# Merging two matrices of a linear-attention layer: the order and shape of the block products

## The chip, the cores and the metric

The kernel runs on one core of one Trainium2 chip. The metric is device time in microseconds of one execution. A core has five engines that run beside each other, each through its own list of instructions: TensorE (PE in the profile; its weight loads are PEld), VectorE (DVE), ScalarE (ACT), GpSimd (POOL) and SyncE (SP), which here issues DMA transfers.

## What is computed

Four layers follow one another, A, B, A, B, each over a sequence of 2048 tokens with 640 features in 32 heads of 20. A is a linear-attention layer, B a layer with softmax attention inside four segments of 512 tokens and a memory across them. The change lies in layer A, which both times runs the same code:

```python
def _A_ref(x, wqkv, wo):                       # x is layer-normed
    qkv = (x @ wqkv).reshape(B, S, 3, H, Dh).transpose(2, 0, 3, 1, 4)
    q, k, v = qkv[0], qkv[1], qkv[2]
    phi = lambda t: jnp.where(t > 0, t + 1, jnp.exp(t)) + 1e-6
    pq, pk = phi(q), phi(k)
    kv = jnp.einsum("bhsd,bhse->bhde", pk, v)
    z = jnp.einsum("bhsd->bhd", pk)
    num = jnp.einsum("bhqd,bhde->bhqe", pq, kv)
    den = jnp.einsum("bhqd,bhd->bhq", pq, z)[..., None] + 1e-6
    o = num / den
    return o.transpose(0, 2, 1, 3).reshape(B, S, D) @ wo
```

## The kernel before

Rows are tiled to 128 partitions (P), the 640 features to five tiles of 128 (C), the sequence to four segments of 512. A matrix of high accuracy is held as an upper and a lower 16-bit part, and a product of two such matrices is three products (upper by upper, upper by lower, lower by upper). Results of 640 columns are made in two halves of 320 (HN), each in a bank of PSUM; `bank()` hands out eight banks in turn.

Layer A never projects v. `g_first` goes through the segments, makes phi of the keys and queries, and sums G = (phi of the keys, transposed) x, in `memory`, whose ten parts are five tiles by two halves. In the last segment (s = 3) it calls `merge`, which turns G into one matrix `wm` that stands for the v projection, the keys' memory and the output projection together. Its stages are, in the order of TensorE's list:

- two steps of `fill`, a generator that holds the four halves of the last two query projections, `queries(2)` and `queries(3)`. A half is 15 products (`proj_n`, L430), an exponential and a relu on ScalarE (`phi_a`), two instructions of VectorE (L445, L747) and a store to DRAM (L748);
- two parts of `memory`, the sums of the keys (L821) with their reciprocals, and the other eight parts of `memory`. VectorE scales G (L837), ScalarE makes the upper copy (L839) and VectorE the lower one (L840), first for the first half of the columns, then for the second;
- one step of `fill`;
- the five inner blocks. Block t is `wv` (tile t of rows) times the scaled G for the heads that touch the tile: heads LO[t] to HI[t], 7 or 8 heads, 140 or 160 columns (L858). VectorE masks the result to the heads' own blocks (L864), ScalarE makes the upper copy in `kt` (L867), VectorE the lower one (L868). A `kt` tile has 512 columns, the block stands from column 128 on, and GpSimd writes zeros on both sides of it (L848, L849). Behind block 1 stands the fourth step of `fill`;
- a further step of `fill`, which by then has nothing left;
- the five outer blocks. Block u is the inner blocks times `wo`. Heads of 20 features do not end at multiples of 128, so beside its own inner block (L888, 128 columns of `kt` as the stationary operand) block u takes a strip of 32 columns of its neighbours' blocks (L894): blocks 0 and 4 have one neighbour, blocks 1 to 3 have two, whose strips are the output rows 0 to 31 and 96 to 127. Each of the two halves has three products per operand, so a block has 6 wide products and 6 or 12 narrow ones. Then ScalarE and VectorE write the two parts of `wm` (L897, L898).

Behind it stands the next stage: `a_head` and `a_second` scale the queries (L929, L933 to L937), transpose them (`turn`, L348) and multiply by `wm` (L430). `merge` runs once at the end of the opening, near 195 to 236 us, and once in the middle, near 1016 to 1054 us. The tile `xo` is the layer's input, loaded again for the sum; `w_Bv` is a weight of layer B, fetched into a buffer that `w_Aq` held.

The order of TensorE's list is the order of the program. The other engines' lists are put in order by a scheduler when the program is built. In the opening GpSimd's queue issues the stores of the queries (L748), later SP's; the weights are always fetched by GpSimd's queue (L300).

Of the kernel before, what the change touches and what calls it, by code (L numbers as in the profile page):

```python
# [20 lines left out]
S, D, H, DH = 2048, 640, 32, 20  # L21
P = 128
C = D // P
# [5 lines left out]
HN = 320  # L29
# [5 lines left out]
LO = [(P * t) // DH for t in range(C)]  # L35
HI = [(P * t + P - 1) // DH for t in range(C)]
# [108 lines left out]
class Kernel:  # L145
# [656 lines left out]
    def merge(self, L, wv, wo, memory, fill):  # L802


        nc, sb = self.nc, self.sb

        def filled(k):
            for _ in range(k):
                x = next(fill, None)
                if x:  # L810
                    yield x

        yield from filled(2)
        for _ in range(2):
            yield next(memory)
        zb = L["z"]
        rz = self.row("rz")
        for n in range(2):
            c = slice(n * HN, (n + 1) * HN)
            p = self.bank()[:, :HN]  # L820
            nc.tensor.matmul(p, self.mhalf.to_broadcast([P, P]), L["z"][:, c], start=True, stop=True)  # L821
            nc.vector.tensor_scalar(zb[:, c], p, -2.0, S * 1e-6, op0=OP.mult, op1=OP.add)
            nc.vector.reciprocal(rz[:, c], zb[:, c])
            nc.vector.tensor_scalar(rz[:, c], rz[:, c], self.k_inv, G_ONE, op0=OP.mult, op1=OP.mult)
            yield 4 * HN * COL
        gs, eps = [], sb.tile([P, C], F32, tag="rca", name="eps", bufs=3)
        for n in range(2):
            for _ in range(C - 2 if n == 0 else C):
                yield next(memory)
            t = self.x_t()  # L830
            gs.append(t)
            for c in range(C):
                e = sb.tile([P, SEG], F32, tag="pq", name="ge", bufs=PQ)[:, :HN]
                if n == 0:
                    nc.vector.tensor_scalar(eps[:, c:c + 1], L["G"][c][:, HN:HN + 1], self.k_scl, 1e-6,
                                            op0=OP.mult, op1=OP.mult)
                nc.vector.scalar_tensor_tensor(e, L["G"][c][:, n * (HN + 1):n * (HN + 1) + HN], eps[:, c:c + 1],  # L837
                                               rz[:, n * HN:(n + 1) * HN], op0=OP.add, op1=OP.mult)
                nc.scalar.activation(t[:, c, 0, :HN], e, AF.Copy)  # L839
                L["parted"] = nc.vector.tensor_tensor(t[:, c, 1, :HN], e, t[:, c, 0, :HN], op=OP.subtract)  # L840
        L["zb"] = zb
        L["pre"] = [self.p_load(L, 0, i) for i in range(3)]
        for _ in memory:
            pass
        yield from filled(1)
        kt = [sb.tile([P, 2, SEG], F16, tag="row", name="kt", bufs=ROWS) for _ in range(C)]
        for t, k2 in enumerate(kt):
            nc.gpsimd.memset(k2[:, :, 64:P], 0.0)  # L848
            nc.gpsimd.memset(k2[:, :, P + (HI[t] + 1 - LO[t]) * DH:320], 0.0)  # L849
        for t, k2 in enumerate(kt):  # L850
            p = self.bank()
            lo, hi = LO[t] * DH, (HI[t] + 1) * DH
            first = True
            for n in range(2):
                a, b = max(lo, n * HN), min(hi, (n + 1) * HN)
                for c in range(C if a < b else 0):
                    for k, m in ((0, 0), (0, 1), (1, 0)):
                        nc.tensor.matmul(p[:, a - lo:b - lo], wv[:, c, k, t * P:(t + 1) * P],  # L858
                                         gs[n][:, c, m, a - n * HN:b - n * HN],
                                         start=first, stop=c == C - 1 and k == 1, skip_group_check=True)  # L860
                        first = False
            e = sb.tile([P, 512], F32, tag="er", name="ke", bufs=3)[:, :hi - lo]
            h = "p (h e) -> p h e"
            nc.vector.scalar_tensor_tensor(e.rearrange(h, e=DH), p[:, :hi - lo].rearrange(h, e=DH), V_SHIFT / G_ONE,  # L864
                                           self.blk[:, OFF[t]:OFF[t] + WID[t]].rearrange(h, e=E1)[:, :, :DH],
                                           op0=OP.mult, op1=OP.mult)
            nc.scalar.activation(k2[:, 0, P:P + hi - lo], e, AF.Copy)  # L867
            L["split"] = nc.vector.tensor_tensor(k2[:, 1, P:P + hi - lo], e, k2[:, 0, P:P + hi - lo], op=OP.subtract)  # L868
            yield 15 * (hi - lo) * COL
            if t == 1:  # L870
                yield from filled(1)
        L["kt"] = True
        for v in L["v"]:
            self.ones_column(v)
        wm = sb.tile([P, C, 2, D], F16, tag="wo", name="wm", bufs=2)
        yield from filled(1)
        halves = [slice(n * HN, (n + 1) * HN) for n in range(2)]
        for u in range(C):
            edges = []
            if u > 0 and (HI[u - 1] + 1) * DH > u * P:  # L880
                edges.append((u - 1, slice(0, 32), 32))
            if u < C - 1 and LO[u + 1] * DH < (u + 1) * P:
                edges.append((u + 1, slice(96, 128), 32))
            ps = [self.bank()[:, :HN] for _ in halves]
            for p, c in zip(ps, halves):
                for k, m in ((0, 0), (0, 1), (1, 0)):
                    a = P + u * P - LO[u] * DH
                    nc.tensor.matmul(p, kt[u][:, k, a:a + P], wo[:, u, m, c], start=k == m, stop=k == 1 and not edges,  # L888
                                     skip_group_check=True)
            for p, c in zip(ps, halves):  # L890
                for k, m in ((0, 0), (0, 1), (1, 0)):
                    for t, r, w in edges:
                        a = P + u * P + r.start - LO[t] * DH
                        nc.tensor.matmul(p[r], kt[t][:, k, a:a + w], wo[:, t, m, c], start=False, stop=k == 1,  # L894
                                         skip_group_check=True)
            for p, c in zip(ps, halves):
                nc.scalar.activation(wm[:, u, 0, c], p, AF.Copy, scale=W_SHIFT)  # L897
                nc.vector.scalar_tensor_tensor(wm[:, u, 1, c], p, W_SHIFT, wm[:, u, 0, c],  # L898
                                               op0=OP.mult, op1=OP.subtract)
                yield 6 * HN * COL  # L900
        L["wm"] = wm
        yield from filled(8)
# [640 lines left out]
```

## Time and profile before

| | us |
|---|---|
| median of 3 runs | 1653.96 |
| lowest and highest of them | 1652.17 and 1654.64 |
| the profiled execution | 1653.39 |
| its span, first to last instruction | 1651.40 |
| TensorE busy | 1613.4 |
| VectorE busy | 1239.5 |

The profile is of one execution. Its span is shorter than its time, because the time has some 2 us around the first and the last instruction. The chain of waits is followed back from the last instruction: at each step to what released it, or to the instruction before it on its engine. Each of its pieces is given with its start, the time that it holds of the chain, and its line.

### The profile page before, as it was taken

To read this page: it belongs to the slowest core of one execution; us is meant where nothing else is said; L and a number is where in the kernel's file an instruction comes from. 1 tells how busy PE (TensorE), PEld (TensorE's weight loads), DVE (VectorE), ACT (ScalarE), POOL (GpSimd) and SP (SyncE) were. 2 spreads that over 40 slices of the span, in tenths; PEclk is the share of its full clock that TensorE was granted. 3 is DMA by queue.
4 is the path that set the end of the run, shared out by engine and by line. 5 is a ranking of instruction groups with operands and counts; after the bars stand their busy time and mean duration, and the time that the engine had idled before them with its cause. 6 is when DMAs were issued, how large, how long until landed. Compare 5 with 4: busy or idle time off the path is not lost.

```text
span 1651.4 us, 37827 instructions
## 1 busy us (share of the span) xinstructions
PE 1613.4 (98%) x13772; PEld 1016.8 (62%) x13772; DVE 1239.5 (75%) x4007; ACT 1015.1 (61%) x1955; POOL 493.0 (30%) x1023
## 2 busy tenths in 40 slices
PE   9999999999999999999999999999999999999998
PEld 6777776654665575556567777756546646645555
DVE  8777794788887797768764556838888878878772
ACT  6877743367667656667666544433775675666773
POOL 3421132023223423433341301210232342332552
PEclk9999999999999999999999999999999999999999
DMA  6444743423322432352211303623232232323422
GB/s 225 160 140 161 275 174 100 134 73 111 96 70 81 142 99 95 108 190 69 66 46 52 102 33 128 214 90 120 77 111 91 100 114 93 109 88 112 147 95 97
DMA packets 110346, 189.32 MB, mean 115 GB/s; under 512 B 14160, under 2 KB 69840, under 8 KB 107728
## 3 DMA queue, kind: packets, MB, share of 16 engines
q1 hardware_dynamic: 97536, 141.02, 26.5%
q0 software_dynamic: 3264, 24.91, 4.1%
q10 hardware_dynamic: 9360, 20.98, 3.3%
q8 instruction: 109, 1.79, 0.5%
q14 instruction: 77, 0.63, 0.1%
HBM read 109.32 MB, written 77.00 MB: 113 GB/s over the span
## 4 chain that ended last, share of the span: by engine, by line
PE 83%; DVE 6%; ACT 5%; DMA 2%; issue 2%; POOL 1%; SPq 0%; ACTq 0%; DVEq 0%; POOLq 0%
PE ps L430 35%; PE ps L416 13%; PE ps L1269 8%; PE ps L757 7%; PE ps L1242 4%; PE ps L348 4%; PE ps L1201 3%; ACT pe L1246 3%; PE ps L472 2%; DVE ps L1207 1%; PE ps L1282 1%; PE ps L1046 1%; PE ps L1056 1%; PE ps L894 1%; DVE oT L353 1%
## 5 line engine op out<-in xcount | busy, mean ns | idle before, releaser
L1207 DVE CUSTOM_DVE_ANT_0 ps<-ps,maskw 128x512 f32<-128x512 f32 (+3 forms) x1024 | 472.3, 520 | 47.3 <-PE ps L1201 43.8
L1246 ACT ACTIVATE pe<-ps,lsc 128x512 f32<-128x512 f32 x640 | 391.9, 695 | 86.1 <-PE ps L1242 68.6
L1253 POOL TENSOR_SCALAR_AFFINE_SELECT pe<-pe 128x256 f32<-128x256 f32 (+1 forms) x640 | 238.3, 380 | 371.7 <-ACT pe L1246 368.8
L430 PEld LDWEIGHTS <-xT 128*128 128x128 f16 x2760 | 267.9, 98 | 104.1 <-issue 5.6
L430 PEld LDWEIGHTS <-oT 128*128 128x128 f16 x1920 | 186.4, 98 | 80.7 <-issue 6.3
L1269 PE MATMUL ps<-pe,v 128*32 128x512 f32 (+3 forms) x2048 | 156.7, 436 | 7.4 <-DVE nat L1017 3.5
L1207 DVE DVE_READ_ACCUMULATOR2_ANT mg<- 128x1 f32 x1024 | 144.6, 141 | 0.0
L430 PE MATMUL ps<-w_Bo,oT 128*128 128x320 f16 x960 | 140.8, 299 | 3.8 <-ACT oT L352 2.4
L416 PE MATMUL ps<-xT,w_Bq 128*128 128x512 f16 x600 | 140.7, 379 | 2.1 <-ACT pe L1246 1.4
L430 PE MATMUL ps<-wm,oT 128*128 128x320 f16 x960 | 142.2, 301 | 0.4 <-DVE mg L1207 0.3
L416 PE MATMUL ps<-xT,w_Bk 128*128 128x512 f16 x600 | 141.6, 379 | 0.4 <-DVE tmp L1292 0.4
L430 PE MATMUL ps<-w_Bv,xT 128*128 128x320 f16 x960 | 139.7, 299 | 0.1
L430 PE MATMUL ps<-w_Aq,xT 128*128 128x320 f16 x960 | 138.1, 299 | 0.6 <-ACT r L444 0.6
L757 PE MATMUL ps<-pk,xs 128*128 128x321 f16 (+1 forms) x960 | 137.0, 300 | 1.5 <-DVE v L777 0.6
L1242 PE MATMUL ps<-qs,ks 62*128 62x384 f16 (+3 forms) x1024 | 131.7, 299 | 4.5 <-ACT pe L1246 2.8
L1017 DVE SCALAR_TENSOR_TENSOR nat<-ps,nat 128x512 f16<-128x512 f32 x80 | 55.2, 690 | 90.0 <-ACT r L1016 67.2
L1201 PE MATMUL ps<-ks,qs 60*128 60x128 f16 (+3 forms) x1024 | 116.6, 297 | 3.5 <-ACT pe L1246 1.7
L430 PE MATMUL ps<-w_Ak,xT 128*128 128x320 f16 x840 | 119.4, 299 | 0.0
L757 PEld LDWEIGHTS <-xs 128*128 128x128 f16 x960 | 93.0, 97 | 39.6 <-issue 2.7
L445 DVE SCALAR_TENSOR_TENSOR e<-e,r 128x320 f32<-128x320 f32 x120 | 60.3, 503 | 73.3 <-ACT r L444 72.7
L1269 PEld LDWEIGHTS ps<-pe,v 128*32 128x32 f32 x2048 | 63.0, 109 | 65.4 <-issue 43.5
L352 ACT ACTIVATE oT<-ps 128x384 f16<-128x384 f32 (+1 forms) x128 | 55.8, 445 | 72.2 <-PE ps L348 57.3
(236 smaller groups left out, 2388.8 us busy)
## 6 DMA issues: line engine op xcount, KB each, us to landing
x<-xn ACTq DMA_DIRECT2D x48, 320.0 KB
qs<-qd SPq DMA_DIRECT2D x128, 120.0 KB
ks<-kd SPq DMA_DIRECT2D x128, 120.0 KB
xo<-x SPq DMA_DIRECT2D x48, 320.0 KB
pqi<-pqd SPq DMA_DIRECT2D x32, 320.0 KB
qd<-nat SPq DMA_DIRECT2D x40, 256.0 KB
kd<-nat SPq DMA_DIRECT2D x40, 256.0 KB
x<-in_A_x SPq DMA_DIRECT2D x16, 320.0 KB
```

Source lines behind the costliest of these rows:

```text
L348: nc.tensor.transpose(pt[:, (c - c0) * P:(c - c0 + 1) * P], src[:, c * P:(c + 1) * P], self.ident)
L352: self.upper = nc.scalar.activation(hi, v, AF.Copy)
L416: nc.tensor.matmul(p, w[:, c, a, t * P:(t + 1) * P], xT[:, c, b, :], start=k == 0, stop=k == 3 * C - 1)
L430: nc.tensor.matmul(p, xT[:, c, a, i * P:(i + 1) * P], w[:, c, b, n * HN:(n + 1) * HN], start=k == 0, stop=k == 3 * C - 1)
L445: nc.vector.scalar_tensor_tensor(e, e, 1.0, r, op0=OP.min, op1=OP.add)
L757: nc.tensor.matmul(p, xs[:, i, a, c * P:(c + 1) * P], pk[i][:, b, cols], start=i == 0 and a == b, stop=i == NT - 1 and a == 1)
L1201: nc.tensor.matmul(bs[par][:, a:a + n], qs[r, p, i * P:(i + 1) * P], ks[r, p, :n], start=True, stop=True)
L1207: nc.vector.tensor_tensor_reduce(bs[par][:, a:a + n], bs[par][:, a:a + n], self.maskw[:, SEG - n:], 1.0, NEG, OP.add, OP.max, G["mg"][:, p ...
L1242: nc.tensor.matmul(b[:, a:a + n], ks[r, p, j * P:(j + 1) * P], qs[r, p, j * P:], start=True, stop=True)
L1246: nc.scalar.activation(e, b, AF.Exp, scale=self.lsc)
L1253: self.select = nc.gpsimd.affine_select(d, d, pattern=pat, compare_op=OP.is_ge, fill=0.0, base=0, channel_multiplier=-1)
L1269: nc.tensor.matmul(G["pv"][32 * h4:32 * h4 + 32, j * P:], v[j][:, h * E1:h * E1 + 32], G.pop((p, par, j)), start=j == 0, stop=j == 2, skip ...
```

## The change

The outer blocks are done in three groups, (0), (1, 2, 3) and (4). A block with one neighbour (0 and 4) takes that neighbour's `kt` in the full width of 128 columns in place of 32. In the group of three, all wide products of the three blocks come first, then all narrow ones, then the writing of `wm`. So that the full-width columns hold zeros where the neighbour has nothing, the fills of `kt` cover all of the first 128 columns and all that is right of the block. And `merge` begins with one step of `fill` in place of two, so that the second half of `queries(2)` comes behind `memory`, the first half of `queries(3)` behind inner block 1, and its second half, at a call that had nothing left before, between the inner and the outer blocks.

```diff
--- before.py
+++ after.py
@@ -810,7 +810,7 @@
                 if x:
                     yield x
 
-        yield from filled(2)
+        yield from filled(1)
         for _ in range(2):
             yield next(memory)
         zb = L["z"]
@@ -845,8 +845,8 @@
         yield from filled(1)
         kt = [sb.tile([P, 2, SEG], F16, tag="row", name="kt", bufs=ROWS) for _ in range(C)]
         for t, k2 in enumerate(kt):
-            nc.gpsimd.memset(k2[:, :, 64:P], 0.0)
-            nc.gpsimd.memset(k2[:, :, P + (HI[t] + 1 - LO[t]) * DH:320], 0.0)
+            nc.gpsimd.memset(k2[:, :, :P], 0.0)
+            nc.gpsimd.memset(k2[:, :, P + (HI[t] + 1 - LO[t]) * DH:], 0.0)
         for t, k2 in enumerate(kt):
             p = self.bank()
             lo, hi = LO[t] * DH, (HI[t] + 1) * DH
@@ -875,25 +875,29 @@
         wm = sb.tile([P, C, 2, D], F16, tag="wo", name="wm", bufs=2)
         yield from filled(1)
         halves = [slice(n * HN, (n + 1) * HN) for n in range(2)]
-        for u in range(C):
-            edges = []
-            if u > 0 and (HI[u - 1] + 1) * DH > u * P:
-                edges.append((u - 1, slice(0, 32), 32))
-            if u < C - 1 and LO[u + 1] * DH < (u + 1) * P:
-                edges.append((u + 1, slice(96, 128), 32))
-            ps = [self.bank()[:, :HN] for _ in halves]
-            for p, c in zip(ps, halves):
+        for us in ((0,), (1, 2, 3), (4,)):
+            edges = {u: [] for u in us}
+            for u in us:
+                if u > 0 and (HI[u - 1] + 1) * DH > u * P:
+                    edges[u].append((u - 1, slice(0, 32)))
+                if u < C - 1 and LO[u + 1] * DH < (u + 1) * P:
+                    edges[u].append((u + 1, slice(96, 128)))
+                if len(edges[u]) == 1:
+                    edges[u] = [(edges[u][0][0], slice(0, 128))]
+            ps = {(u, n): self.bank()[:, :HN] for u in us for n in range(2)}
+            for (u, n), p in ps.items():
                 for k, m in ((0, 0), (0, 1), (1, 0)):
                     a = P + u * P - LO[u] * DH
-                    nc.tensor.matmul(p, kt[u][:, k, a:a + P], wo[:, u, m, c], start=k == m, stop=k == 1 and not edges,
-                                     skip_group_check=True)
-            for p, c in zip(ps, halves):
+                    nc.tensor.matmul(p, kt[u][:, k, a:a + P], wo[:, u, m, halves[n]], start=k == m,
+                                     stop=k == 1 and not edges[u], skip_group_check=True)
+            for (u, n), p in ps.items():
                 for k, m in ((0, 0), (0, 1), (1, 0)):
-                    for t, r, w in edges:
-                        a = P + u * P + r.start - LO[t] * DH
-                        nc.tensor.matmul(p[r], kt[t][:, k, a:a + w], wo[:, t, m, c], start=False, stop=k == 1,
-                                         skip_group_check=True)
-            for p, c in zip(ps, halves):
+                    for t, r in edges[u]:
+                        a = P + u * P - LO[t] * DH
+                        nc.tensor.matmul(p[r], kt[t][:, k, a + r.start:a + r.stop], wo[:, t, m, halves[n]], start=False,
+                                         stop=k == 1, skip_group_check=True)
+            for (u, n), p in ps.items():
+                c = halves[n]
                 nc.scalar.activation(wm[:, u, 0, c], p, AF.Copy, scale=W_SHIFT)
                 nc.vector.scalar_tensor_tensor(wm[:, u, 1, c], p, W_SHIFT, wm[:, u, 0, c],
                                                op0=OP.mult, op1=OP.subtract)
```

## Rows read from the trace of the kernel before

**Rows 1.** the page: busy time and share by engine; shares of the chain that ended last.

```profile
PE 1613.4 (98%) x13772; PEld 1016.8 (62%) x13772; DVE 1239.5 (75%) x4007; ACT 1015.1 (61%) x1955; POOL 493.0 (30%) x1023
...
PE 83%; DVE 6%; ACT 5%; DMA 2%; issue 2%; POOL 1%; SPq 0%; ACTq 0%; DVEq 0%; POOLq 0%
```

**Rows 2.** chain of waits, first merge: start us, us, engine, line, instructions.

```profile
223.38 2.90 PE ps L858 x60
226.28 0.81 PE ps L888 x6
227.10 0.92 PE ps L894 x6
...
228.94 1.19 PE ps L894 x12
...
231.05 1.13 PE ps L894 x12
...
235.86 1.02 PE ps L348 x8
...
239.35 2.04 PE ps L430 x15
...
250.63 0.55 PE ps L348 x5
```

**Rows 3.** the same chain, second merge.

```profile
1044.59 0.81 PE ps L888 x6
...
1049.09 0.96 PE ps L894 x12
...
1053.73 1.02 PE ps L348 x8
```

**Rows 4.** busy us (count) of PE, PEld, DVE, ACT, POOL; clock, DMA share, GB/s.

```profile
195.00:205.00 10.00, 10.00 (x71) 7.10 (x70) 7.18 (x20) 5.91 (x15) 3.02 (x10) 1.00 1.01 376
205.00:215.00 10.00, 10.00 (x74) 7.02 (x72) 10.00 (x23) 3.64 (x6) 4.69 (x3) 1.00 0.16 64
215.00:225.00 10.00, 10.00 (x121) 8.19 (x119) 10.00 (x26) 6.09 (x17) 2.27 (x10) 1.00 0.24 67
```

**Rows 5.** timeline, first merge, VectorE, GpSimd: start us, us, engine, line, operation, out<-in.

```profile
221.54 1.36 DVE L840 TENSOR_TENSOR xT<-ge,xT 128x320 f16<-128x320 f32 x3
...
222.82 0.49 DVE L445 SCALAR_TENSOR_TENSOR e<-e,r 128x320 f32<-128x320 f32 x1
...
223.43 0.32 DVE L747 TENSOR_SCALAR e<-e 128x320 f32<-128x320 f32 x1
...
227.76 1.60 DVE L868 TENSOR_TENSOR kt<-ke,kt 128x160 f16<-128x160 f32 x1
...
229.98 1.27 POOL L937 TENSOR_TENSOR pqi<-pqi,rca 128x640 f32<-128x640 f32 x1 [0.81 <-DVE rca L935]
230.02 1.39 DVE L868 TENSOR_TENSOR kt<-ke,kt 128x140 f16<-128x140 f32 x1
...
231.80 0.24 DVE L868 TENSOR_TENSOR kt<-ke,kt 128x140 f16<-128x140 f32 x1
```

**Rows 6.** timeline, GpSimd, first merge; two lines by source and tile (min/median/max ns).

```profile
216.38 0.20 POOL L848 MEMSET kt<- 128x128 f16 x1 [4.63 <-PE ps L757]
...
224.62 0.55 POOL L300 DMA_DIRECT2D w_Bv<-wd_Bv  x1
...
L1005 POOL MEMSET ks<- x3: 951/951/951, 249.7 to 251.5; 128x1024 f16 x3
...
L430 PE MATMUL ps<-w_Bv,xT x960: 296/299/310, 255.6 to 1446.2; 128*128 128x320 f16 x192
```

**Rows 7.** timeline, second merge, VectorE and SP's queue.

```profile
1040.25 0.95 DVE L840 TENSOR_TENSOR xT<-ge,xT 128x320 f16<-128x320 f32 x2
...
1047.07 10.55 SPq L359 DMA_DIRECT2D xo<-x  x3
...
1048.17 1.11 DVE L868 TENSOR_TENSOR kt<-ke,kt 128x140 f16<-128x140 f32 x1 [0.30 <-ACT kt L867]
```

## The prediction

> **What bounds the kernel now.** I read the page first: TensorE is busy for 98% of the span, and of the chain that ended last it holds 83% [rows 1]. So a microsecond taken from TensorE's own list shows in the end time wherever TensorE is the engine that is waited for, and only there. The change touches one function, `merge`, which runs twice, so I read the chain of waits through both places next [rows 2, 3]. The reader is to see that the chain is TensorE alone, one line after the other without a piece of another engine: sixty products of the last three inner blocks (L858, 2.90 us), then the outer blocks (L888 and L894 by turns), then the transposes of the next stage (L348). The first outer stage lasts from 226.28 to 235.86, 9.58 us; the second from 1044.59 to 1053.73, 9.14 us. Last comes what TensorE has to wait for, if it gets faster: VectorE, which makes the operands. In the three stretches around the first merge it is busy 7.18, 10.00 and 10.00 of 10 us [rows 4]: it is full from about 205 on and has room only before. That is the point on which the prediction turns.
>
> **What a turn of shape costs.** Each of the five outer blocks is now done as 6 products with a stationary of 128 columns (L888), then 6 or 12 with 32 columns (L894). The very first 6, which follow products of their own shape, take 0.81 us; the next 6 narrow ones take 0.92 [rows 2]. The other pieces of these lines, nine in a merge, are 0.92 too, but for three with a wait in them (1.19 and 1.13 in the first merge, 0.96 in the second) [rows 2, 3]. Two readings follow. First, twelve narrow products take no longer than six wide ones, so the two strips of an inner block (output rows 0 to 31 and 96 to 127) run beside each other, and a pair costs one slot of 0.81/6 = 0.136 us. Second, each change of shape costs 0.92 - 0.81 = 0.11, by the unrounded slots 0.105 us. The tenth change stands at the end: eight transposes behind a narrow piece take 1.02 us, five in the middle of wide work 0.55, so eight would be 0.88 [rows 2]; the surplus, 0.14, is the same size.
>
> **Part 1, the outer blocks.** Blocks 0 and 4 have one neighbour each; that neighbour's product is now taken over all 128 columns, most of them zero, so its 6 products cost 6 slots as before and no change of shape. Blocks 1 to 3 do their 18 wide products in one go and then their 36 narrow ones, which are 18 pairs. Slots before: 60; after: 12 + 18 + 18 + 12 = 60. The slots don't change, only the turns do: ten before, two after (into the narrow run and out of it). I price a turn at 0.105: 8 x 0.105 = 0.84 us a merge, 1.68 in all. The outer stage becomes 60 x 0.136 + 2 x 0.105 = 8.37 us.
>
> **Part 2, the waits.** In the first merge the two pieces of 1.19 and 1.13 hold 0.27 and 0.21 us of waiting beyond 0.92, for the lower copies of inner blocks 2 and 3 (L868), which VectorE ends late, at 229.36 and 231.41: two of the three took 1.60 and 1.39 us, where one took 0.24 [rows 5]. The second merge waits 0.04 [rows 3]. Half a query projection, 15 products, is 2.04 us of TensorE [rows 2]. It moves from ahead of the keys' product with x to behind it, and the later halves move on by one place each, so that the last stands between the inner and the outer blocks. The sum on TensorE is nil. But the inner blocks now end 2.04 us earlier while the outer ones begin at the same time, which gives their copies 2.04 us more. If that works, 0.48 + 0.04 = 0.52 us of waits go.
>
> Does it work? What comes ahead of the inner blocks is 2.04 us shorter on TensorE, and VectorE has to follow. Its full stretch begins with the sums that this moves forward, so it can begin up to 2.04 earlier, in the room before 205. It now takes the moved half's evacuation (0.49 + 0.32 = 0.81 us, L445 and L747 [rows 5]) in the full stretch, and loses the last half's 0.81 only if that is put behind the copies. So the lower copy of block 3 comes at 231.41 - 2.04 = 229.37, or at 230.18. The new order wants it earlier than the old one: the wide product of block 3 starts 24 slots into the stage and uses it in its third product, at 226.28 + 3.26 + 0.27 = 229.81. The wait is 0 or 0.37. In the second merge the same copy ends at 1049.28 [rows 7], less 2.04 is 1047.24, or 1048.05; it is wanted at 1044.59 + 3.53 = 1048.12, so no wait. I take 0.2 us of new wait in all, the middle for the first merge.
>
> **Part 3, the zeros.** The fills of `kt` (L848, L849) grow from 128 and 104 elements in a partition to 256 and 488: 512 more for each of the five tiles. A fill of 1024 elements takes 0.951 us on GpSimd [rows 6], so 0.48 us a tile, 2.4 us a merge. They are off the path: even the late ones stand at 216.38 [rows 6], ten microseconds ahead of the outer blocks that read them. What they can cost is VectorE's time. The rows show both: L868 at 1.60 and, beside GpSimd's L937 of 1.27, at 1.39, but 0.24 alone [rows 5]. The fill is a write without a tensor input, nearer to nothing than to that; the bounds are 0 and the late two tiles' 0.95 us, and I take 0. The Trainium skill has a rule against this part ("GPSIMD Engine Reference", section "Specifications"): GpSimd shares its SBUF interfaces with VectorE, and VectorE instructions with two SBUF inputs contend. L868 is such an instruction and agrees; for a fill no run here shows it, and by the rule the sum would carry the 0.95 of the bound.
>
> **Part 4, the queues.** The moved halves also store to DRAM (L748). In the first merge GpSimd issues these, and behind the third half's store stands the fetch of `w_Bv` at 224.62, whose tile is free only after the last query half; that half now ends up to 2.9 us later (the length of L858's piece), and the fetch with it. The first product with `w_Bv` is at 255.6 [rows 6], 31 us behind the old issue and 28 behind the new one, so the fetch is covered. In the second merge SP issues the stores, and the loads of `xo` at 1047.07 are behind them in its queue [rows 7]; they wait for the last half's VectorE work, some half a microsecond more, and are first read in the next stage. Both at nothing.
>
> **The sum.** Turns -1.68, waits -0.52, new wait +0.20: -2.0 us. The profiled execution took 1653.39 us (1651.40 of span, 1.99 around it), so it would take 1651.4; it lies 0.57 below the median of the runs, 1653.96, so the median goes to **1652.0 us**. What 0.2% is here, 3.3 us, is about what a measurement of this kernel can tell from no change; my sum is below it.
>
> **Rival 1: VectorE doesn't come forward, and TensorE waits for it** (slower). Its place is ahead of inner block 2, which now starts at 223.38 - 2.04 = 221.34 and needs the second half's last lower copy (L840) about 0.9 us later, at 222.24; before, that copy ended at 222.90 [rows 5]. If VectorE's end stays where it is, TensorE waits 0.66 there, then 0.94 more for block 3's copy: 1.60, against 0.84 + 0.48 gained, +0.28 net. In the second merge L840 ends at 1041.20 [rows 7], wanted at 1040.55: 0.65, then 0.51, net +0.28. With the moved 0.81 added and the fills' 0.95 as well, the first wait is 2.42 and the second 0.94 in the first merge, 2.41 and about 0.5 in the second: +2.0 each. So +0.6 to +4.0, in the middle +2.3: 1656.3 us; it passes 0.2% only at the upper end. It decides from the point where L840 ends later than about 0.9 us after block 2's first product. For it: VectorE at 10.00 of 10. Against it: 2.8 of 10 us free before 205, where the moved sums land. 18%.
>
> **Rival 2: the turns aren't what costs 0.11**, so that the change doesn't do what it says. If the surplus belongs to the start of each new group in a bank and not to the shape, the ten starts stay or grow, and only the waits go: -0.52 + 0.20 = -0.3, 1653.6 us. Against it: L430 starts a new bank after each 15 products, and two halves in a row take 2.04 us each, 15 slots with nothing over. 7%.
>
> **How the numbers follow.** Forecast 60%, rival 1 18%, rival 2 7%. The remaining 15% are for the order of VectorE, ScalarE and GpSimd, which isn't written out by hand and is drawn anew for the whole program when the list changes; no row prices it, and I split it nearly evenly. Faster by over 0.2%: 8% of these and 2% from the forecast's spread, 10%. Slower: 7%, and 4% from rival 1's upper end, 11%. Within: 79%. The range starts at the forecast without new wait, 1651.8, less the runs' own spread of 1.8 below the median, 1650.0; it reaches over rival 2 and the middle of rival 1 to 1656.4.
>
> **What would show it.** Right: in each merge six products of 0.81 become one piece of twelve, then 18, 36 and 12, with two surpluses of a tenth; the outer stage lasts near 8.4 us; no wait for L868; the last query half ends just before it. Wrong: idle time of TensorE ahead of L858's second group or inside L888 with L840 or L868 as its releaser (rival 1); narrow pairs that no longer run beside each other, which would add 18 slots, 2.4 us a merge; or a different length in stages that the change doesn't touch.

## The result, and the profile after

Over 22 runs of each, taken beside each other, the changed kernel takes 1655.66 us (1650.97 to 1660.52) and the kernel before 1652.67 (1650.68 to 1654.64). The ratio is 1.0016 [1.0010, 1.0022], with its 95% interval in brackets: slower by 2.7 us, 1.7 to 3.6. The forecast was 1652.0, two microseconds below the kernel before. The time lies in the range, near its upper end, and on the other side of the kernel before than the forecast. So something of some five microseconds isn't in the sum.

The profiled execution took 1656.31 us, with a span of 1654.3. TensorE's busy time is 1.3 us less than in [rows 1], the chain has nearly the same shares, but for one of its lines that was not there, a transfer (`DMA pqi<-pqd`):

```profile
PE 1612.1 (97%) x13772; PEld 1018.3 (62%) x13772; DVE 1239.7 (75%) x4007; ACT 1016.1 (61%) x1955; POOL 498.3 (30%) x1023
...
PE ps L430 35%; PE ps L416 13%; PE ps L1273 9%; PE ps L757 7%; PE ps L1246 4%; PE ps L348 4%; PE ps L1205 3%; ACT pe L1250 3%; PE ps L472 2%; DVE ps L1211 2%; PE ps L1286 1%; DMA pqi<-pqd 1%; PE ps L1050 1%; PE ps L1060 1%; DVE oT L353 1%
```

(In the changed kernel the lines behind the outer blocks' products have moved on: L888 is L891, L894 is L897, L897 and L898 are L901 and L902, L919 is L923, L929 to L937 are L933 to L941.)

The chain of waits of the changed kernel through the first merge, which answers to [rows 2] (start us, us, engine, line, instructions):

```profile
226.51 0.81 PE ps L891 x6
227.32 0.81 PE ps L897 x6
228.14 2.44 PE ps L891 x18
230.58 2.55 PE ps L897 x36
233.13 0.92 PE ps L891 x6
234.05 0.81 PE ps L897 x6
234.87 0.87 PE ps L348 x8
```

This is what the prediction drew: the first twelve products without a surplus, 18, 36 and then 12, a tenth in 2.55 and in 0.92, no wait. The stage lasts 234.87 - 226.51 = 8.36 us where it lasted 9.58. VectorE is in time (its timeline, to be read against [rows 5]):

```profile
220.99 0.49 DVE L840 TENSOR_TENSOR xT<-ge,xT 128x320 f16<-128x320 f32 x1
...
225.45 1.50 DVE L938 TENSOR_SCALAR rca<-rca 128x32 f32<-128x32 f32 x1
...
228.55 0.30 DVE L868 TENSOR_TENSOR kt<-ke,kt 128x140 f16<-128x140 f32 x1 [0.15 <-ACT kt L867]
229.39 0.49 DVE L445 SCALAR_TENSOR_TENSOR e<-e,r 128x320 f32<-128x320 f32 x1 [0.27 <-ACT r L444]
```

The last copy of the second half of G (L840) ends at 221.48, where 222.24 was the point from which TensorE would wait. The last lower copy of an inner block (L868) ends at 228.85, and only behind it, from 229.39 on, comes the evacuation of the last query half.

The chain through the second merge, which answers to [rows 3], begins in the same manner and then leaves TensorE for a transfer of 12.78 us:

```profile
1041.71 0.81 PE ps L891 x6
...
1045.79 0.53 PE ps L897 x6
...
1046.34 0.85 ACT wm L901 x2
...
1047.23 12.78 DMA pqi<-pqd
...
1060.04 0.83 DVE pqi L933
1060.86 0.34 DVE oT L353
...
1061.25 0.71 PE ps L430 x2
...
1062.39 3.19 PE ps L430 x15
```

The transfer is the load of a query tile: `a_second` reads the fourth tile of the first segment back from DRAM (L923), to scale, transpose and multiply it by `wm`. SP's queue and VectorE's timeline of the same stretch show both ends of it:

```profile
1037.17 9.89 SPq L748 DMA_DIRECT2D pqd<-e  x3
1047.23 0.32 SPq L923 DMA_DIRECT2D pqi<-pqd  x1
```

```profile
1050.99 1.34 DVE L353 TENSOR_TENSOR oT<-ps,oT 128x384 f16<-128x384 f32 x3
1060.04 0.83 DVE L933 TENSOR_TENSOR pqi<-pqi,z 128x640 f32<-128x640 f32 x1 [7.71 <-DMA pqi<-pqd]
1060.78 0.42 DVE L353 TENSOR_TENSOR oT<-ps,oT 128x256 f16<-128x256 f32 x1
```

VectorE stands for 7.71 us, with the second piece of an evacuation (L353) queued behind, and TensorE for 3.71 at a product that needs that piece. In the kernel before the same load is issued 0.5 us earlier, and the tile is read 3.7 us later than VectorE now comes to it (1056.04 and 1052.33), without a wait. These are times from the start of each trace; the changed kernel's is 2.88 us ahead at the first outer product already (1041.71 and, in [rows 3], 1044.59). SP's queue and VectorE's timeline of the kernel before:

```profile
1046.70 0.32 SPq L919 DMA_DIRECT2D pqi<-pqd  x1
```

```profile
1056.04 0.81 DVE L929 TENSOR_TENSOR pqi<-pqi,z 128x640 f32<-128x640 f32 x1
```

What this costs can be read from TensorE's timelines. The transposes after the outer blocks start at 1049.91, in the kernel before at 1053.66: 3.75 us ahead. The fifth group of 15 products with `wm` starts at 1065.75, in the kernel before at 1064.05: 1.70 behind. So 5.45 us are lost in between. They aren't all waiting: after the wait TensorE's granted clock falls. Busy time by engine, then the clock, in stretches of 4 us of the changed kernel:

```profile
1052.00:1056.00 4.00, 4.00 (x32) 3.09 (x31) 0.33 (x1) 0.52 (x2) 0.00 (x0) 1.00 1.05 436
1056.00:1060.00 4.00, 1.54 (x12) 0.88 (x9) 0.00 (x0) 0.35 (x1) 0.00 (x0) 1.00 0.86 355
1060.00:1064.00 4.00, 2.75 (x11) 1.78 (x12) 3.96 (x10) 0.07 (x1) 0.69 (x1) 0.65 0.06 25
```

The 15 products in the stretch of 0.65 take 3.19 us in the chain, where 2.04 is their time elsewhere. 3.71 of waiting, 1.2 there and 0.2 in the two transposes ahead are 5.1 of the 5.45 us; the two products at the end of the wait hold the rest. The trace also shows that DMA works at its mean busy share of 1.05 and 0.86 while VectorE waits: the tile of 320 KB is on its way beside weights of 1600 KB, `w_Bq`, issued at 1046.48, 0.75 us ahead of the tile's load, and `w_Bk`, issued at 1050.38. In the kernel before, `w_Bq` goes out 4.42 us behind that load. GpSimd's timeline of the changed kernel, then of the kernel before:

```profile
1046.48 0.59 POOL L300 DMA_DIRECT2D w_Bq<-wd_Bq  x1
```

```profile
1051.12 0.59 POOL L300 DMA_DIRECT2D w_Bq<-wd_Bq  x1
```

### The profile page after: what moved, and what is told of

The parts are those of the page before. It is cut to its first block, busy times and chain, and to the rows that moved or that the text cites. A ratio compares the mean times of both kernels' runs of the same rounds, so it can differ in the third digit from the quotient of the medians.

```text
span 1654.3 us, 37814 instructions
## 1 busy us (share of the span) xinstructions
PE 1612.1 (97%) x13772; PEld 1018.3 (62%) x13772; DVE 1239.7 (75%) x4007; ACT 1016.1 (61%) x1955; POOL 498.3 (30%) x1023
## 4 chain that ended last, share of the span: by engine, by line
PE 83%; DVE 6%; ACT 6%; DMA 2%; issue 2%; POOL 1%; SPq 0%; ACTq 0%; DVEq 0%; POOLq 0%
PE ps L430 35%; PE ps L416 13%; PE ps L1273 9%; PE ps L757 7%; PE ps L1246 4%; PE ps L348 4%; PE ps L1205 3%; ACT pe L1250 3%; PE ps L472 2%; DVE ps L1211 2%; PE ps L1286 1%; DMA pqi<-pqd 1%; PE ps L1050 1%; PE ps L1060 1%; DVE oT L353 1%
## 5 line engine op out<-in xcount | busy, mean ns | idle before, releaser
L430 PEld LDWEIGHTS <-xT 128*128 128x128 f16 x2760 | 267.8, 98 | 103.9 <-issue 5.6
L430 PEld LDWEIGHTS <-oT 128*128 128x128 f16 x1920 | 186.7, 98 | 85.3 <-issue 6.3
L430 PE MATMUL ps<-wm,oT 128*128 128x320 f16 x960 | 142.2, 301 | 4.1 <-DVE oT L353 3.7
L430 PE MATMUL ps<-w_Bo,oT 128*128 128x320 f16 x960 | 142.0, 301 | 3.9 <-ACT oT L352 2.4
L430 PE MATMUL ps<-w_Bv,xT 128*128 128x320 f16 x960 | 139.7, 299 | 0.1
L430 PE MATMUL ps<-w_Aq,xT 128*128 128x320 f16 x960 | 138.4, 299 | 0.6 <-ACT r L444 0.6
L1205 PE MATMUL ps<-ks,qs 60*128 60x512 f16 (+3 forms) x1024 | 116.2, 297 | 3.6 <-ACT pe L1250 1.7
L430 PE MATMUL ps<-w_Ak,xT 128*128 128x320 f16 x840 | 119.4, 299 | 0.0
```

Source lines behind the costliest of these rows:

```text
L430: nc.tensor.matmul(p, xT[:, c, a, i * P:(i + 1) * P], w[:, c, b, n * HN:(n + 1) * HN], start=k == 0, stop=k == 3 * C - 1)
L1205: nc.tensor.matmul(bs[par][:, a:a + n], qs[r, p, i * P:(i + 1) * P], ks[r, p, :n], start=True, stop=True)
```

## The experiments

My theory after the two traces: the gain of the change is there, all of it, and is eaten by the fourth query tile, which SP can issue only behind the store of the last query half, and whose reader now comes earlier. The rivals: the moved half or the fills cost something themselves; or the transfer is late because of the weights beside it, and its place in the queue is of no account; or the loss is spread over the whole program by the new order of the other engines.

**The new shape alone.** The groups and the fills of the change, but two steps of `fill` ahead as before:

```diff
-        yield from filled(1)
+        yield from filled(2)
```

> The regrouped outer blocks and the longer zero fills alone; the query half stays ahead of the keys' product. Theory 1 (the loss is the fourth query tile, L923, landing late in the second merge because the moved half brings the weight fetches forward): no wait for a DMA in the second merge, eight turns of 0.105 us less in each merge (-1.7 us in all), of which the waits for L868 take back up to 1.6 and 1.2 us; so between -1.7 and +1.1 us against before, about 0. Rival (the regrouping itself loses the time, by the banks held for three blocks or by the fills): 2 to 3 us slower than before, with TensorE waiting inside the outer stage.

Measured: 1654.67 us, the kernel before beside it 1652.84; ratio 1.0006 [0.9997, 1.0014]. No wait for the tile. TensorE's timeline of the first merge shows what the moved half is for:

```profile
227.98 1.25 PE L891 MATMUL ps<-w_Ak,kt 128*128 128x320 f16 x8
229.65 1.07 PE L891 MATMUL ps<-w_Ak,kt 128*128 128x320 f16 x6 [0.42 <-DVE kt L868]
231.69 0.72 PE L891 MATMUL ps<-w_Ak,kt 128*128 128x320 f16 x4 [0.98 <-DVE kt L868]
```

The wide products of blocks 1 to 3, in one go, want the copies of blocks 2 and 3 earlier than the old order did, and TensorE waits 1.4 us for them, in the second merge 0.9. A merge comes out 0.4 to 0.5 us longer than before. Where the copies stay put and only the order changes, rival 1's arithmetic gives waits of 1.60 and 1.16 us and +0.28 a merge; these are a little shorter. The regrouping alone is no gain. Its tile's load is issued at 1046.97, 4.42 us ahead of `w_Bq`, as in the kernel before.

**The moved half alone.** The kernel before with one step of `fill` ahead:

```diff
-        yield from filled(2)
+        yield from filled(1)
```

> The moved query half alone; outer blocks and fills as before. Theory 1: the wait for the fourth query tile in the second merge is there too; its reader comes 0.8 us later than in the changed kernel, so it waits some 3 us instead of 3.7, and the clock falls behind it; with 0.5 us of waits for L868 gone, 1 to 3 us slower than before. Rival (the regrouping loses the time): 0.5 us faster than before, with no wait for a DMA.

Measured: 1653.96; ratio 1.0005 [0.9996, 1.0014]. The chain through the first merge has every piece at 0.92, and the two of 1.19 and 1.13 of [rows 2] are gone:

```profile
228.79 0.92 PE ps L894 x12
...
230.63 0.92 PE ps L894 x12
```

In the second merge the load of the tile is issued at 1047.78, behind the store and 0.75 us behind `w_Bq`, and VectorE waits 1.65 us for it: the late load comes with the moved half. TensorE, for which I expected a wait of some 3 us, has none. VectorE comes to the tile 0.9 us later after its issue than with the regrouping (6.0 in place of 5.1), but the larger part is that the tile landed in 7.6 us in place of 12.8. Why it landed sooner here stays open.

**The load ahead.** The changed kernel with the fourth tile's load ahead of the outer blocks, so that it stands ahead of the last stores in SP's queue:

```diff
+        L["fourth"] = self.p_load(L, 0, 3)
         wm = sb.tile([P, C, 2, D], F16, tag="wo", name="wm", bufs=2)
...
-                yield from self.p_read(L, s, i + 3, o)
+                yield from self.p_read(L, s, i + 3, o, L["fourth"] if s == 0 else None, nc.vector)
```

> The changed kernel, with the load of the fourth query tile put in the program ahead of the outer blocks, so that SP issues it with the first three and not behind the last half's store. Theory 1: the wait for the tile and the half clock behind it go; what the trace of after gains up to there, 1.4 us in the first merge and 0.9 in the second, stays, so 2 to 3 us faster than before, near 1650.3 us, and the spread of the runs narrows. Rival (the regrouping, or a new order of the other engines elsewhere): as slow as the changed kernel, 2 to 3 us above before.

Measured: 1652.06; 0.9997 [0.9988, 1.0006]. The load is issued at 1030.24 and nobody waits for it. But the scaling of the tile, ready early, is now put ahead of copies of `wm` on VectorE, and TensorE waits 1.0 us for these (L892 for L903).

**The fetches later.** The changed kernel with the fetches of `w_Bq` and `w_Bk` held back behind the scaling of the fourth tile, and SP's order as it was:

```diff
-            nc.gpsimd.tensor_tensor(q3, q3, rc[:, :, None].to_broadcast([P, H, DH]), op=OP.mult)
+            self.scaled = nc.gpsimd.tensor_tensor(q3, q3, rc[:, :, None].to_broadcast([P, H, DH]), op=OP.mult)
...
-            for k in "vq":
-                wB[k] = self.fetch(("B", k))
+            wB["v"] = self.fetch(("B", "v"))
...
-                    wB["k"] = self.fetch(("B", "k"))
+                    with self.tc.issue_after(self.scaled.ins):
+                        for k in "qk":
+                            wB[k] = self.fetch(("B", k))
```

> The changed kernel, with the fetches of w_Bq and w_Bk issued behind the fourth query tile's rescaling, so that none of them runs beside that tile's load; SP's order is untouched, the load is still issued behind the last half's store near 1047 us. If the fetches make the load late (12.8 us to land), it lands in 3 to 6 us, at the time it is wanted (1051) or 2 us later: 1 to 2.5 us faster than before. If only its late place in SP's queue counts, it lands near 1057 to 1060 as now and the kernel stays 2 to 3 us slower than before.

Measured: 1651.98; 1.0000 [0.9992, 1.0009]. The tile is issued at 1048.59, later than in any other kernel, and VectorE reads it at 1053.61 without waiting: it landed in at most 5.0 us, where it took 12.8 beside the two fetches. So the weights beside it do make it slow. But the fetches, now at 1058.98 and 1060.13, make another load late. VectorE waits for the fourth row tile of `xo`, issued at 1061.47, long after the store, and landed 11.07 us later by the chain, and TensorE waits 1.1 us for an operand that hangs on it (L348 for L403). VectorE's timeline:

```profile
1072.63 0.55 DVE L498 SCALAR_TENSOR_TENSOR xn<-ps,ioG,xo 128x320 f32<-128x320 f32 x1 [3.84 <-DMA xo<-x]
```

**The load ahead, the scaling behind the copies.** As the third, with the scaling held behind the copies of `wm`:

```diff
-                nc.vector.scalar_tensor_tensor(wm[:, u, 1, c], p, W_SHIFT, wm[:, u, 0, c],
+                L["copied"] = nc.vector.scalar_tensor_tensor(wm[:, u, 1, c], p, W_SHIFT, wm[:, u, 0, c],
...
-        with self.tc.issue_after(L["split"].ins):
+        with self.tc.issue_after(L.get("copied", L["split"]).ins):
```

> The early load of the fourth query tile again, and VectorE's rescaling of that tile put behind the lower copies of wm, where it stood before; ahead of them it made TensorE wait 1.05 us for a bank in the second merge of the early-load kernel. Theory 1 (the late tile, and nothing else, eats the gain): no wait of TensorE from the first outer block to the end of the next stage in either merge, so both merges keep their 1.4 and 0.9 us: 2 to 3 us faster than before, near 1650.5 us. Rival (something outside the merges takes the rest of the gain, since the early load alone came out only 0.8 us below before): again within 1 us of before, with the merges free of waits.

Measured: 1651.40 (1649.69 to 1659.28); 0.9997 [0.9984, 1.0010]. In the profiled execution TensorE waits nowhere in the two merges, but seven runs lie at 1649.7 to 1651.7 and five at 1655.2 to 1659.3. The same kernel, run once more:

> The kernel with the early load and the ordered rescaling a second time, for a closer interval and a second trace. Theory 1: no wait of TensorE in either merge and the stages behind them, the outer stages 8.36 us each; 1 to 3 us faster than before. Rival (the fewer waits are luck of one execution): a wait in or behind one of the merges, and a time within 0.5 us of before or above it.

Measured: 1653.02 (1651.20 to 1658.53); 1.0002 [0.9993, 1.0011]. Its profiled execution shows the next one in the row. VectorE's timeline, then TensorE's:

```profile
1058.38 0.55 DVE L498 SCALAR_TENSOR_TENSOR xn<-ps,ioG,xo 128x320 f32<-128x320 f32 x1 [5.03 <-DMA xo<-x]
...
1058.93 0.42 DVE L353 TENSOR_TENSOR oT<-ps,oT 128x256 f16<-128x256 f32 x1
```

```profile
1059.41 0.45 PE L430 MATMUL ps<-wm,oT 128*128 128x320 f16 x2 [2.28 <-DVE oT L353]
```

The rows `xo` are the next load behind the same store: issued at 1046.63, landed at 1058.28 by the chain. In the first execution of this kernel VectorE waited 2.6 us for them and TensorE had enough in hand; here it is 5.0, and TensorE waits 2.28. So taking one load out of the queue only hands the wait to the next. In the time, the rivals' expectations were met in both measurements (ratios of 0.9997 and 1.0002), and not mine of 1 to 3 us. What the late tile and the late `xo` have in common is the store ahead of them in SP's queue, and `w_Bq` fetched just before them; the experiments with the store on another queue, below, take up the first.

**The kernel before with the load ahead.** The third's edit on the kernel before:

> The kernel before with the early load alone. Theory 1: before, the tile is in time (its rescaling at 1056.04 waits for no DMA), so the early load gains nothing: within 0.7 us of before, or up to 1 us slower where the rescaling, now ahead of the copies of wm, makes TensorE wait for a bank. Rival (the early load is a gain of its own, and says nothing on the change): 1 to 3 us faster than before.

Measured: 1652.50; 0.9998 [0.9989, 1.0006]. The load isn't late there, and taking it out of the queue gives nothing.

**The changed kernel again**, beside these:

> The changed kernel a second time, beside the two others. Theory 1: 2 to 4 us above before; the fourth tile needs 7 to 13 us to land beside the weight fetches, so the wait behind it differs from execution to execution: in the profile between 0 and 4 us, and the runs spread over more than those of before. Rival (a fixed wait or a fixed order is the cause): a wait of 3.5 to 4 us in the profile as in the first one.

Measured: 1654.50; 1.0010 [1.0001, 1.0018]. VectorE waits 7.1 us for the tile, TensorE 3.1 for VectorE: the wait isn't one execution's.

**A turn's price.** The fifth kernel with the three middle blocks one by one, but the neighbours of blocks 0 and 4 in full width: six turns in place of two.

```diff
-        for us in ((0,), (1, 2, 3), (4,)):
+        for us in ((0,), (1,), (2,), (3,), (4,)):
```

> The same kernel, but blocks 1, 2 and 3 done one after the other, each with its wide and then its narrow products: six turns of shape in a merge in place of two, the same products and banks. If a turn costs 0.105 us, the outer stage lasts 60 x 0.136 + 6 x 0.105 = 8.79 us where no copy is waited for, and the four added pieces are longer by a tenth each. If the surplus belongs to the start of a group in a bank and not to the shape, the stage lasts as long as with the three blocks together, 8.36 us.

Measured, one execution: 1656.06 us. The chain through its first merge:

```profile
227.25 0.81 PE ps L898 x6
228.06 0.81 PE ps L892 x6
228.88 0.92 PE ps L898 x12
```

From TensorE's timeline the stage lasts 235.06 - 226.27 = 8.79 us, in the second merge 1053.60 - 1044.81 = 8.79 too: 0.43 more than 8.36 for four more turns, 0.107 each. A new group in a bank that keeps the shape takes 0.81; only the change of shape takes 0.92. So rival 2 is out.

**The store on another queue.** The smallest edit on the suspected cause: of the changed kernel, the store of the very last query half is issued by GpSimd and no longer by SP. The lists of TensorE, VectorE and ScalarE are the changed kernel's.

```diff
-                (self.q_pq if L["early"] else nc.sync).dma_start(L["pqd"][s][i][:, n * HN:(n + 1) * HN], e)
+                (self.q_pq if L["early"] or (s, i, n) == (NSEG - 1, NT - 1, 1) else nc.sync).dma_start(L["pqd"][s][i][:, n * HN:(n + 1) * HN], e)
```

> The changed kernel with one store moved to another queue: in the second merge the last query half's store (L748) is issued by GpSimd in place of SP; the lists of TensorE, VectorE and ScalarE stay as they are. The theory (the fourth query tile and the x rows come late because they stand behind that store on SP) expects SP to issue the fourth tile's load at about 1042, behind the store before, in place of 1047.2; it is then on the chip before VectorE wants it at 1052.3, VectorE's wait of 7 us and TensorE's of 3 to 3.7 us are gone, the first x row is there in time too, and the time comes 2 to 3 us below the changed kernel's, at 1651 to 1652.5, the forecast. The rival (the transfers are late because of the weight fetches beside them, wherever they are issued) expects the tile to be late again, by more than 3 us, and 1654 to 1655. What the move may cost: GpSimd waits for VectorE's last half at 1046.7 with two rescalings behind that store, so the second would end at about 1048 and the third at 1049.5, in place of 1044.2 and 1046.5; they are wanted at about 1050 and 1052.

Measured: **1649.97 us** (1647.95 to 1652.31), the kernel before beside it 1652.69; ratio 0.9984 [0.9975, 0.9993]. It is faster than both, by a little more than I expected. SP's queue, GpSimd's and VectorE's timelines:

```profile
1036.85 4.44 SPq L748 DMA_DIRECT2D pqd<-e  x2
1041.46 0.32 SPq L923 DMA_DIRECT2D pqi<-pqd  x1
```

```profile
1045.06 0.55 POOL L748 DMA_DIRECT2D pqd<-e  x1 [3.75 <-DVE e L747]
1045.62 2.51 POOL L941 TENSOR_TENSOR pqi<-pqi,rca 128x640 f32<-128x640 f32 x2
1048.07 0.58 POOL L300 DMA_DIRECT2D w_Bq<-wd_Bq  x1
```

```profile
1051.92 0.82 DVE L933 TENSOR_TENSOR pqi<-pqi,z 128x640 f32<-128x640 f32 x1
...
1054.60 0.54 DVE L498 SCALAR_TENSOR_TENSOR xn<-ps,ioG,xo 128x320 f32<-128x320 f32 x1
```

The load is issued 5.8 us earlier than in the changed kernel, neither the tile nor `xo` is waited for, and TensorE waits nowhere in the stretch. The fetch of `w_Bq` comes 1.6 us later than in the changed kernel, as its place is behind the store; `w_Bk` keeps its time. So the edit moves two things: the loads come earlier, and one fetch later. For the tile the earlier load suffices: with the load ahead, and `w_Bq` where it was, nobody waited for it. For `xo` the two are not separated. As TensorE, VectorE and ScalarE work in the changed kernel's order, that order isn't what costs the time. The rescalings that I feared for end at 1048.13 instead of 1049.5, in time.

**The same move on the kernel before, and once more on the changed one**, beside each other:

> The kernel before with the same store moved from SP to GpSimd. The theory (in the kernel before the fourth tile, issued at 1046.7, is read at 1056.0 without a wait for it) expects no change: 1652 to 1653.5, ratio to before within 0.999 to 1.001. GpSimd's three rescalings, at 1044.7 to 1051.2, would stand behind a store at about 1046 and end up to 1.5 us later, without TensorE waiting for them for more than 0.5. The rival (moving the store is worth 2.7 us by itself, whatever the order of the change) expects about 1650.

> The changed kernel with the store moved, a second time, beside the kernel before with the same store moved. If its 0.9984 [0.9975, 0.9993] stands, 1649.5 to 1651 and an interval that ends below 1; if that was a lucky draw, 1652 and an interval around 1.

Measured: on the kernel before 1653.77, ratio 1.0003 [0.9994, 1.0012]; on the changed one 1650.03, ratio 0.9983 [0.9974, 0.9992], the kernel before beside both 1653.05. In the profiled execution of the latter VectorE waits 1.9 us for the third row tile of `xo`, issued at 1053.43, behind both fetches, and TensorE waits nowhere between 1036 and 1075. On the kernel before the load then goes out at 1041.14, and this changes nothing; the move is worth something only together with the change. So 1649.97 and 1650.03 are the change's own worth without its queue: 2.7 and 3.0 us less than the kernel before, and 5.7 (1655.66 - 1649.97) less than with it, or 4.5 by the changed kernel's second measurement (1654.50).

## Why the prediction was wrong, point by point

**The turns of shape: right.** 8.37 us was forecast for the outer stage, 8.36 was measured in both merges, and the price of a turn by itself is 0.107, forecast 0.105.

**The waits for the copies: right, and needed.** Both are gone. The regrouping without the moved half has new ones (1.4 and 0.9 us), near the 1.60 and 1.16 of rival 1's arithmetic. The new wait of 0.2 a run that I allowed for is nil: the last copy ends at 228.85, a little before the earlier of my two values, 229.37.

**The moved half's VectorE work: right.** L840 ends at 221.48, 0.76 ahead of the point where rival 1 decides. In the first merge VectorE's list puts the last half behind the copies, which was the better of the two cases.

**The zeros: right at nothing.** GpSimd's late fills, those of two tiles, stand at 214.72 to 216.19, beside four L840 of VectorE. GpSimd's timeline and VectorE's:

```profile
214.72 0.31 POOL L848 MEMSET kt<- 128x256 f16 x1
214.97 0.51 POOL L849 MEMSET kt<- 128x488 f16 x1
```

```profile
214.51 1.69 DVE L840 TENSOR_TENSOR xT<-ge,xT 128x320 f16<-128x320 f32 x4
```

Four in 1.69 are 0.42 each; the three at 221.54 in the kernel before, without a fill beside them, are 0.45 each (1.36 in all, [rows 5]). The 0.95 of the bound is not there. I had read the rule of the Trainium skill too widely; another of its pages is narrower ("SBUF — State Buffer", section "Who interferes with whom"): a VectorE instruction with two SBUF inputs contends with a GpSimd instruction that reads SBUF, and not with one that only writes it. The trace agrees with this: beside these fills L840, with its two inputs, keeps its length, and beside GpSimd's rescaling, which reads, L868 takes 1.39 [rows 5].

**The sum: right.** The two outer stages became shorter by 1.22 us (9.58 to 8.36) and, with the store moved, by 0.78 (9.14 to 8.36; 1041.38 to 1049.74 in that kernel's chain). This is 2.0. The tenth turn stands behind the stage, in the transposes, which went from 1.02 to 0.87 in both merges, so 2.3 in all; the prediction's sum had 2.2 without its new wait, which didn't come. The measured 2.7 [1.2, 4.1] and 3.0 agree.

**The queues: wrong. This is the step that failed**: "Both at nothing." I had seen that SP's loads stand behind the last half's store. Four things were wrong or not priced.

First, the store's delay. I took "some half a microsecond", and the trace times seem to agree: the fourth tile's load went out at 1047.23, where it was 1046.70. That is chance. Counted from the first outer product the load goes out at 5.52 us (1047.23 - 1041.71), where it went out at 2.11 (1046.70 - 1044.59): 3.4 later. 2.9 of these are the sixty products of L858, behind which the last half now stands. I had named them for the first merge and left them out for the second. The rest is VectorE's work. The lead of 2.88 us that hides this is not the change's alone: 1.1 of it are there behind the first merge (236.92 and 235.78, the starts of L430), and the kernel before then loses some 1.7 at a low clock near 332 (below), where the changed kernel loses nothing.

Second, I named only the `xo` loads as what waits behind the store; the query tile's load (L919) stood between the store and them.

Third, I put the readers "in the next stage" and left it at that, without a time. Counted in the same way, VectorE came to the tile at 11.45 and now comes at 10.62, 0.83 earlier. So the 9.3 us from the issue to the reader became 5.1, and the store's new place took four fifths of the difference.

Fourth, the price of the load wasn't taken from a row. The moved half also brings GpSimd's third rescaling forward, and with it `w_Bq` behind it: from 6.53 to 4.77 us behind the first outer product. So the load left 4.42 us ahead of `w_Bq` and now leaves 0.75 behind it. The kernel with the moved half alone has the same 5.52 and 4.77. 320 KB landed in at most 5.0 us without `w_Bq` and `w_Bk` beside them, in 7.6 with them there, and in 12.8 with them in the changed kernel. Against 5.1 us this is a wait of nothing, of 2.5 or of 7.7; the last is the measured one itself.

**The chances.** Slower by over 0.2% had 11%, of which 7 were for the order of the other engines and none for the queues. The measured +0.16% lies within what I called the same, on the other side of the kernel before than the sum. In hindsight, a rival that names this place, with the forecast's 1652.0 and TensorE's wait of 3.7, would have given 1655 to 1656.

What stays open is the scatter. In all profiled executions but one (the fetches later), one to three stretches ahead of the program's end have a low granted clock, each behind a stretch in which TensorE was partly idle, and the places differ from kernel to kernel and between executions of one kernel. In the kernel before, in stretches of 4 us:

```profile
328.00:332.00 4.00, 3.10 (x50) 1.56 (x47) 3.35 (x10) 1.94 (x4) 0.72 (x2) 1.00 0.21 82
332.00:336.00 4.00, 3.83 (x28) 2.27 (x17) 3.81 (x17) 0.70 (x2) 0.00 (x0) 0.57 0.16 48
```

In the changed kernel this is at 1060 and 1596, in its second profiled execution only near 1596, in the one with the load ahead and its scaling held back at 1352 and 1592. A stretch of 4 us at 0.57 costs 1.7 us ((1 - 0.57) x 4). That spreads the times by as much as the change is worth, and I can't say for each kernel how much of its time is due to it.

## What to carry to other kernels

A change that moves a store changes the time that every load behind it in its queue has, also of loads that the change doesn't touch. List these loads, and for each take the time from its new issue to its reader and set it against the longest landing under the transfers that will then run beside it. Count such times from one instruction that stands in both traces, not from the start of each trace: here a lead of 2.9 us between the traces hid most of a delay of 3.4. When a change whose parts all show in the trace as forecast doesn't show in the time, look for the first stretch in which the lead over the old trace gets smaller. And mend a late load at the instruction that holds its queue: here, moving the load alone handed the wait to the next in the queue, and holding back the fetches beside it handed it to a load further on.

## What the runs showed of the hardware

- A tile of 320 KB landed in 12.8 us beside two weights of 1600 KB, in 7.6 beside the same two in the kernel with the moved half alone, and in at most 5.0 with both held back. In this last kernel the two fetches run later, and a row tile of `xo` of the same size landed in 11.1 beside them.
- GpSimd's rescaling (L941, two tensor inputs) stretches VectorE's instructions beside it also where these have one tensor input: L938 from 0.17 to 1.50 (at 225.45), and L747 from 0.32 to 1.28 at 1045.44, which delayed the last store itself by almost 1 us; in the kernel before the same L747 takes 1.16, and 0.33 in the changed kernel with the store moved, where the rescaling comes behind it. Both are of the operation TENSOR_SCALAR; the section "Who interferes with whom" of the Trainium skill's "SBUF — State Buffer" names it among those that can contend, under conditions on their operands.
- After the wait of 3.71 us at a granted clock of 1.00, the next 4 us were granted 0.65: of the two levels, 2.4 and 1.2 GHz, the lower for most of it. The 15 products took 3.19 us, the next 15 again 2.04.
